# The place of two operand copies in the opening of a gated attention and GEGLU kernel

## The chip, the cores and the metric

The kernel runs on 1 core of one Trainium2 chip. The metric is device time in microseconds (us). Before the change the median of 3 runs was 596.25 us (595.72 to 597.62). The profile comes from one further execution, which took 596.87 us, with a span of 595.1 us from its first to its last instruction and a granted TensorE clock of 0.999.

The engines are named as in the profile: PE is TensorE's matmul and PEld its weight load, DVE is VectorE, ACT is ScalarE, POOL is GpSimd, SP is SyncE with its DMA queue.

## The reference

For 2048 tokens of width 512 the kernel mixes two branches with a gate per token:

```python
x = A_x
g = _sigmoid((x * gate_w).sum(-1, keepdims=True))
a = _A_ref(x, A_wqkv, A_wo)
b = _B_ref(x, B_w_gate, B_w_up, B_w_down)
return g * a + (1 - g) * b
```

Branch a projects x to queries, keys and values (32 heads of width 16). Each position attends to 8 positions, itself and every second one behind it; the result is projected with wo. Branch b is a GEGLU feed-forward layer of width 1792. All is float32.

## The kernel before

**Products.** Large matrix products are made from seven products of blocks instead of eight: x is cut in four blocks (a11, a12, a21, a22), a weight in four (b11, b12, b21, b22), and sums of blocks (s1 to s4 of x, t1 to t4 of the weight) are multiplied. `KEYS` lists the seven pairs for keys and queries: a11 x b11, a12 x b21, s2 x t2, s3 x t3, a22 x t4, s1 x t1, s4 x b22. Each operand of float32 is split in a high part, a copy to the type fp32r, and a low part, the raw value less the high part; a product of two operands is then three matmuls (high x high, low x high, high x low), for each of two chunks `kc` of the inner dimension. A copy of the high part is an ACT instruction, the low part a DVE subtraction.

**Token tiles and banks.** A block of x has four token tiles (`BT = 4`), and each tile of a product has a PSUM bank, 128 x 512. Products follow one another in the same bank: partial sums are evicted by an ACT copy when they stand for a result, and the next product accumulates on top.

**The opening** is written out at L1055 to L1197. The first two key products fill the banks `acc0` to `acc3` (`C`) and four `p` banks (`Z_`). `third(k)` (L1154) makes key product number k of `KEYS` on `C`, counted from 0: `third(2)` is the third product, s2 x t2; `third(3)` the fourth, s3 x t3; `third(4)` the fifth, a22 x t4. In `third`, each token tile's matmuls (`key_mm`, L454 to L461) are followed for k = 2 and 3 by an eviction on ACT (L1164) into a staging tile `hh` or `hl`, and by two stores on the SP queue (`store_b`, L463); for k = 4 by `take_first` (L320). The value products of the opening (`values`, L336, matmuls at L348) are interleaved: two of them ahead of `third(2)`, the others after the key products, beginning with s1 x t1.

**Copies and subtractions of the opening.** `late_split` (L1106) copies an operand's high part on ACT (L1108) and puts its low part on a list `low`; `lows(n)` (L1111) takes the first n from the list and issues their subtractions on DVE (L1114). `late_s` makes a sum of x, `late_b` a sum of the weight, both by `late_split`. In the profile t4's raw input is the tile `prod` and its parts lie in a tile `g` (g<-prod); s1's raw input is `lg` and its parts are in `S` (S<-lg); a22's parts are in `A`. `make_v` (L160) makes the operands of the value products in steps, taken one by one with `next(made)`: a copy at L87, a subtraction at L88, sums at L168.

**What sets the order.** A planner orders the instructions of each engine from the order of the text, their dependences and an estimated clock; an instruction whose inputs come early can go ahead of one that stands earlier in the text. Each engine then takes its instructions in the planned order. Two means hold an instruction: `tc.keep_in_program_order(ins)` puts `ins` behind the instruction of the same engine that precedes it in the text, without a wait of its own on the chip; `paced(ins)` (L581) does the same for DVE instructions while `PIN[0]` is true, which it is from L1073 to L1194, and ties an instruction to the last matmul while `PACING[0]` is true. ACT's copies of the opening have no hold.

**Later stages.** After the opening come the rest of the value products, the feed-forward loop of the first half of the tokens (`ffn(0)`, matmuls at L730 and L777) with the attention's DVE work spread over it (L519, L522, L558), then keys and values of the second half (`keys`, L416, and `values`), `ffn(1)` and the output. Weight operands `g` of the feed-forward layer are partly split by a DMA that adds raw to a negated copy (L689, issued from POOL, g<-raw).

## Time and profile before

| | us |
|---|---|
| runs, median of 3 | 596.25 (595.72 to 597.62) |
| profiled execution | 596.87 |
| its span | 595.1 |
| PE busy in the span | 586.6 |
| DVE busy | 533.3 |
| ACT busy | 429.4 |
| POOL busy | 123.4 |

The profile's views are read thus. The page gives busy time by engine. The list of waits gives, for an engine's line, what it waited for, the total, the number of times and the longest. A timeline is in the order of time, with equal neighbours merged: start and duration in us from the span's start, engine, line, operation, output<-input, shape, count, and in brackets the idle time of the engine before it with what ended it. A window gives the busy time of PE, PEld, DVE, ACT and POOL in a stretch, the granted clock, the mean busy share of the DMA engines and GB/s. The chain of waits follows back from the last instruction what released each step. A matmul's duration overlaps that of the next one, so steps of PE are read from start to start.

### The profile page before, as it was taken

The numbers are of one execution on the slowest core, as the hardware profiler recorded it, in microseconds if no ns is written. First come the engines' busy times: TensorE is split into PE (matmuls) and PEld (weight loads), VectorE is DVE, ScalarE is ACT, GpSimd is POOL, SyncE is SP. The second block draws the span as 40 slices with busy tenths as digits, with TensorE's granted clock in tenths as the row PEclk, the third lists the DMA queues.
The fourth block names the chain that finished last, engine by engine and source line by source line (L and its number), as shares of the span: only waits on it lengthen the run. The fifth ranks groups of instructions, "written<-read, shape, count | busy, mean of one in ns | idle before, by whom it ended". The sixth has DMA issues, their size and how long they took to land.

```text
span 595.1 us, 8276 instructions
## 1 busy us (share of the span) xinstructions
PE 586.6 (99%) x2743; PEld 488.8 (82%) x2743; DVE 533.3 (90%) x622; ACT 429.4 (72%) x758; POOL 123.4 (21%) x144
## 2 busy tenths in 40 slices
PE   9999999999999999999999999999999999999997
PEld 7889887888888888887788888888888888888885
DVE  6989898999799996999996999799979988999891
ACT  6778786678887779777767665767696778796632
POOL 0130670112111112112001571112121212141200
PEclk9999999999999999999999999999999999999999
DMA  8689999989878988899889999889778988988725
GB/s 301 223 235 295 307 284 236 295 245 243 260 219 246 232 268 234 237 344 267 255 264 330 258 276 227 230 190 265 198 247 213 260 213 215 265 197 230 98 53 176
DMA packets 89464, 143.28 MB, mean 241 GB/s; under 512 B 8655, under 2 KB 49999, under 8 KB 89422
## 3 DMA queue, kind: packets, MB, share of 16 engines
q1 hardware_dynamic: 67470, 106.91, 54.6%
q0 software_dynamic: 21664, 35.46, 33.8%
q8 instruction: 21, 0.34, 0.3%
q10 hardware_dynamic: 288, 0.39, 0.2%
q14 instruction: 21, 0.17, 0.1%
HBM read 69.83 MB, written 46.49 MB: 195 GB/s over the span
## 4 chain that ended last, share of the span: by engine, by line
PE 90%; DMA 6%; DVE 1%; ACT 1%; issue 1%; SPq 0%; ACTq 0%; DVEq 0%
PE p L730 42%; PE p L777 13%; PE acc L777 12%; PE acc L460 10%; PE p L1002 5%; PE acc L348 3%; PE p L348 3%; DMA g<-raw 2%; PE acc L1002 2%; DMA v<-vs 1%; DMA raw<-ws 1%; PE p L460 1%; DMA vs<-hh 1%; DMA raw<-xt 1%; DVE raw L245 1%
## 5 line engine op out<-in xcount | busy, mean ns | idle before, releaser
L730 PE MATMUL p<-S,g 128*128 128x512 f32 x672 | 166.7, 389 | 0.0
L730 PEld LDWEIGHTS p<-S,g 128*128 128x128 f32 x672 | 126.0, 188 | 26.1
L730 PE MATMUL p<-A,g 128*128 128x512 f32 x504 | 125.1, 390 | 0.7 <-DMA g<-raw 0.7
L730 PEld LDWEIGHTS p<-A,g 128*128 128x128 f32 x504 | 94.3, 188 | 20.8 <-DMA g<-raw 1.1
L558 DVE TENSOR_TENSOR prod<-v,lg 128x2048 f32<-128x2048 f32 x32 | 72.9, 2279 | 0.8
L519 DVE TENSOR_TENSOR prod<-kq 128x2048 f32<-128x2048 f32 x32 | 72.9, 2278 | 0.6 <-DMA kq<-kq 0.3
L522 DVE TENSOR_REDUCE lg<-prod 128x128 f32<-128x2048 f32 x32 | 73.0, 2281 | 0.1
L777 PE MATMUL p<-d,hh 128*128 128x512 f32 x224 | 68.8, 389 | 0.0
L689 POOL DMA_DIRECT2D g<-raw x27 | 23.4, 867 | 188.9 <-ACT g L686 122.9
L741 ACT ACTIVATE c<-p 128x512 f32<-128x512 f32 x56 | 33.3, 597 | 38.9 <-PE p L730 38.6
L777 PE MATMUL acc<-d,hh 128*128 128x512 f32 x224 | 58.4, 390 | 0.0
L777 PEld LDWEIGHTS acc<-d,hh 128*128 128x128 f32 x224 | 42.0, 188 | 8.9 <-ACT hh L749 0.2
L777 PEld LDWEIGHTS p<-d,hh 128*128 128x128 f32 x224 | 42.1, 188 | 8.7
L742 DVE TENSOR_TENSOR c<-c,s 128x512 f32<-128x512 f32 x56 | 37.8, 683 | 5.6 <-ACT c L741 5.4
L777 PE MATMUL p<-d,hl 128*128 128x512 f32 x112 | 42.6, 389 | 0.0
L746 DVE TENSOR_TENSOR c<-c 128x512 f32<-128x512 f32 x56 | 38.3, 684 | 3.2 <-ACT c L843 3.1
L562 DVE TENSOR_TENSOR prod<-prod 128x1024 f32<-128x1024 f32 x32 | 39.1, 1221 | 0.3
L735 ACT ACTIVATE s<-p 128x512 f32<-128x512 f32 x56 | 33.0, 590 | 7.1 <-PE p L730 6.5
L721 POOL DMA_DIRECT2D d<-r x23 | 19.7, 858 | 86.6 <-ACT d L720 60.0
L460 PE MATMUL acc<-d,S 128*128 128x512 f32 x144 | 35.2, 390 | 0.6 <-ACT hh L1164 0.6
L790 ACT ACTIVATE rt<-p 128x512 f32<-128x512 f32 x48 | 28.1, 594 | 9.4 <-PE p L777 9.1
L777 PE MATMUL acc<-d,hl 128*128 128x512 f32 x112 | 34.5, 389 | 0.0
(220 smaller groups left out, 1065.0 us busy)
## 6 DMA issues: line engine op xcount, KB each, us to landing
g<-raw POOLq DMA_DIRECT2D x27, 512.0 KB, 6.1
ws<-g SPq DMA_DIRECT2D x14, 768.0 KB, 5.9
g<-ws SPq DMA_DIRECT2D x14, 768.0 KB, 7.0
r<-wff SPq DMA_DIRECT2D x28, 256.0 KB, 4.5
raw<-wff SPq DMA_DIRECT2D x14, 512.0 KB, 4.5
d<-r POOLq DMA_DIRECT2D x23, 256.0 KB, 6.5
ws<-raw SPq DMA_DIRECT2D x14, 384.0 KB, 4.9
raw<-ws SPq DMA_DIRECT2D x14, 384.0 KB, 4.9
```

What stands on the lines that cost most here:

```text
L348: LAST[:] = [nc.tensor.matmul(ps[:, :n], x[:, ts], VO[b][w][:, kc * WQ:kc * WQ + n], start=first, stop=(kc == 1 and i == 2), skip_group_ch ...
L460: LAST[:] = [nc.tensor.matmul(ps, x[:, ts], w, start=(start and kc == i == 0), stop=(kc == 1 and i == 2), skip_group_check=True)]
L519: paced(nc.vector.tensor_tensor(prod, spans(k, jj), q[:, jj:jj + 2, None, :].to_broadcast([P, 2, W, UC]), op=OP.mult))
L522: nc.vector.tensor_reduce(two_of(lg, jj), prod.rearrange("p j w (h d) -> p (j w) h d", d=DH), axis=AX.X, op=OP.add)
L558: paced(nc.vector.tensor_tensor(prod.rearrange("p j w (h d) -> p (j w) h d", d=DH), spans(v, jj).rearrange("p j w (h d) -> p j w h d", d=D ...
L562: nc.vector.tensor_tensor(prod[:, :, :4], prod[:, :, :4], prod[:, :, 4:], op=OP.add)
L730: LAST[:] = [nc.tensor.matmul(ps, w_, a_, start=(start and kc == 0 and n == 0), stop=(kc == 1 and n == 2), skip_group_check=True)]
L741: nc.scalar.activation(c, ps, AF.Copy)
L742: nc.vector.tensor_tensor(c, c, s, op=OP.add)
L746: nc.vector.tensor_tensor(ge, ge, up, op=OP.mult)
L777: LAST[:] = [nc.tensor.matmul(pp, a[:, ts], w, start=(i == 0 and n == 0 and gr == 0), stop=(i == 1 and n == 2), skip_group_check=True)]
L1002: LAST[:] = [nc.tensor.matmul(pa, a, b, start=(first and n == 0), stop=(last and n == 2), skip_group_check=True)]
```

## The change

`late_split`, `late_s` and `late_b` take an optional hold for the high part's ACT copy. t4's two copies are given `tc.keep_in_program_order`; the ACT instruction ahead of the first in the text is the last eviction of `third(2)`. The call of `third(3)` is moved ahead of the s1 copies, which get the same hold; the ACT instruction ahead of the first of them is then the last eviction of `third(3)`. The subtractions of t4, a22 and s4, which were issued three and three around the s1 copies, are issued together ahead of `third(3)`. Those of s1 follow, as before, with `lows(len(low))` after the next step of `made`.

```diff
-    def late_split(name, kc, x):
+    def late_split(name, kc, x, hold=lambda ins: ins):
         hi, lo, raw = x
-        nc.scalar.activation(hi, raw, AF.Copy)
+        hold(nc.scalar.activation(hi, raw, AF.Copy))
         low.append((lo, raw, hi))
...
-    def late_s(n, kc):
+    def late_s(n, kc, *hold):
         i = {"s1": 3, "s2": 0, "s4": 1, "s3": 2}[n]
         raw = S1.pop(kc) if n == "s1" else XR[kc][:, i * 512:(i + 1) * 512]
         XOP[n, kc] = pair("S")
-        late_split(n, kc, (*XOP[n, kc], raw))
+        late_split(n, kc, (*XOP[n, kc], raw), *hold)
 
-    def late_b(n, kc):
-        late_split(n, kc, (*QO[n, kc], QR[n, kc]))
+    def late_b(n, kc, *hold):
+        late_split(n, kc, (*QO[n, kc], QR[n, kc]), *hold)
...
     for kc in range(2):
         combine_b("t4", "b21", "b21", "t2", kc)
-        late_b("t4", kc)
+        late_b("t4", kc, tc.keep_in_program_order)
         lows(1)
     for kc in range(2):
         late_split("a22", kc, (*X[0, 1, 2 + kc], XR[kc][:, 1536:]))
         sum_x(kc, "s4")
         late_s("s4", kc)
     set_x(0)
-    lows(3)
+    lows(min(6, len(low)))
+    third(3)
     for kc in range(2):
-        late_s("s1", kc)
-    lows(3)
-    third(3)
+        late_s("s1", kc, tc.keep_in_program_order)
     room_v(*LARGE)
     store_v()
     next(made)
```

## The prediction

> **What bounds the kernel now.** I read the page's busy shares first, then the list of what TensorE waited for, then the timelines of TensorE, ScalarE and VectorE around the edited lines, and last the chain of waits.

> ```profile
> span 595.1 us, 8276 instructions
> ...
> PE 586.6 (99%) x2743; PEld 488.8 (82%) x2743; DVE 533.3 (90%) x622; ACT 429.4 (72%) x758; POOL 123.4 (21%) x144
> ```

> TensorE (PE) is busy for 586.6 of 595.1 us. An edit to the order of the other engines can win only where it closes a gap of PE, and all its gaps together are 8.5 us. The waits of PE over the whole run, with the total, the number of times and the longest:

> ```profile
> PE p L730 <- DMA g<-raw: 0.7, 1, 0.7
> PE p L460 <- ACT p L434: 0.6, 1, 0.6
> PE acc L460 <- ACT hh L1164: 0.6, 1, 0.6
> PE acc L348 <- ACT hh L355: 0.5, 1, 0.5
> PE acc L460 <- ACT S L129: 0.4, 1, 0.4
> ```

> The third row is the opening's: a matmul of the key products (L460) waits once for an eviction (L1164). PE's timeline there (start, duration, engine, line, output<-input, count, and the idle time before it with what ended it), and then ScalarE's (ACT):

> ```profile
> 26.55 1.08 PE L460 MATMUL acc<-g,S 128*128 128x512 f32 x4
> 28.26 5.75 PE L460 MATMUL acc<-d,S 128*128 128x512 f32 x24 [0.62 <-ACT hh L1164]
> 33.84 5.60 PE L460 MATMUL acc<-g,A 128*128 128x512 f32 x24
> 39.28 3.44 PE L348 MATMUL p<-g,S 128*128 128x512 f32 x24
> ```

> ```profile
> 27.08 0.63 ACT L1108 ACTIVATE g<-prod 128x512 fp32r<-128x512 f32 x1
> 27.60 0.60 ACT L1164 ACTIVATE hh<-acc 128x512 f32<-128x512 f32 x1
> ...
> 29.04 0.63 ACT L1164 ACTIVATE hl<-acc 128x512 f32<-128x512 f32 x1
> 29.51 0.67 ACT L87 ACTIVATE g<-tb 128x516 fp32r<-128x516 f32 x1
> 30.04 0.67 ACT L1108 ACTIVATE g<-prod 128x512 fp32r<-128x512 f32 x1
> ...
> 31.08 0.64 ACT L1164 ACTIVATE hh<-acc 128x512 f32<-128x512 f32 x1
> ...
> 32.07 1.20 ACT L1108 ACTIVATE S<-lg 128x512 fp32r<-128x512 f32 x2
> 33.12 0.64 ACT L1164 ACTIVATE hl<-acc 128x512 f32<-128x512 f32 x1
> ...
> 34.07 0.67 ACT L1164 ACTIVATE hl<-acc 128x512 f32<-128x512 f32 x1
> 34.55 0.71 ACT L87 ACTIVATE g<-v 128x516 fp32r<-128x516 f32 x1
> ```

> The four rows of PE are the end of the third key product, the fourth (s3 x t3), the fifth (a22 x t4) and the value product s1 x t1. The third ends at 26.55 + 1.08 = 27.63. Its first eviction (27.60) stands on ACT behind one copy, t4's first (g<-prod, 27.08), and the fourth product, which goes on in the bank that is evicted, begins only at 28.26. PE stands for 0.62 us. The reader is to see that a copy needed only by the fifth product, at 33.84, went ahead of an eviction for which PE was waiting.

> **The change part by part.** No instruction is added, removed or resized. The two copies that get a hold issue no DMA, and the fourth product's stores keep their place among those of the Sync queue. What moves is the order of ACT's copies, and in the text the fourth product goes ahead of the s1 copies. VectorE's subtractions keep their sequence: two for t4, four for a22 and s4, then t1's, then two for s1.

> First edit: t4's first copy behind the third product's last eviction. That copy kept the eviction from ACT from 27.08 to 27.60, start to start, so 0.52 us. Without it the eviction takes the place at 27.08. From the eviction's start to PE's start it was 28.26 - 27.60 = 0.66 us, so the fourth product begins at 27.74, a gain of 0.52. The bounds: PE cannot gain more than the 0.62 us that it stood, and it gains nothing if another ready copy takes the free place. I take 0.52, since the eviction's input is there: of the four matmuls from 26.55 on the first ends about 0.4 us later (the 5.60 us row less 23 steps of 0.227, the step being (39.28 - 33.84) / 24), near 26.95. The second t4 copy has the hold too, but the ACT instruction ahead of it in the text is the first one, so its hold adds only their sequence.

> What becomes late is t4's copy itself. It now follows the fourth eviction, which moves from 29.04 to 28.52, so it starts near 29.04 instead of 27.08. Its subtraction stands on VectorE (DVE) ahead of others:

> ```profile
> 28.88 0.68 DVE L1114 TENSOR_TENSOR g<-prod,g 128x512 fp32r<-128x512 f32 x1
> 30.74 0.69 DVE L1114 TENSOR_TENSOR g<-prod,g 128x512 fp32r<-128x512 f32 x1 [1.18 <-ACT g L1108]
> ...
> 32.55 0.68 DVE L1114 TENSOR_TENSOR A<-raw,A 128x512 fp32r<-128x512 f32 x1
> ...
> 35.29 0.70 DVE L88 TENSOR_TENSOR g<-v,g 128x516 fp32r<-128x516 f32 x1 [0.85 <-ACT g L87]
> ...
> 40.70 0.70 DVE L88 TENSOR_TENSOR g<-tb,g 128x516 fp32r<-128x516 f32 x1 [0.90 <-ACT g L87]
> ```

> It goes from 28.88 to about 29.7, and the 1.18 us for which DVE stood before 30.74 covers these 0.8 us. The second t4 copy (30.04) has the same ACT work ahead of it as before: four evictions, t4's first copy, the value weight's copy of 29.51. So 30.74 and what follows stay. The fifth product reads them. It would begin at 33.84 - 0.52 = 33.32, and its fifth matmul, at 33.32 + 4 x 0.227 = 34.23, is the first that needs the second a22 low, done at 32.55 + 0.68 = 33.23: 1.0 us of cover. Beyond it every further us would stop PE one for one.

> Second edit: the s1 copies (32.07, two of them) go behind the eviction of 34.07, which moves to 33.55, so to 34.1, or to 34.6 if the value copy of 34.55 goes ahead of them. The eviction of 33.12 comes earlier, for which nobody waits: the fifth product comes to its bank at 33.32 + 6 x 0.227 = 34.68. The price is on DVE. If the s1 copies go first, t1's subtraction (35.29) comes about 0.5 us later, and the two of s1 behind it end at 37.6 instead of 37.1 (35.29 and three of 0.6). PE needs them from 39.28 - 0.52 = 38.76: 1.1 us of cover. Further down the 0.90 us for which DVE stood before 40.70 takes up the 0.5; without it the 0.5 would be paid. I take nothing, with 0 and +0.5 as the ends. The hold also keeps the s1 copies, whose inputs are early, from taking the place that t4's copy leaves.

> The sum at the opening is -0.52 + 0 + 0. It has to last to the end. The chain of waits shows the one place of the first hundred microseconds behind it where PE does not lead:

> ```profile
> 67.30 4.89 DMA vs<-hh
> ...
> 72.61 8.25 DMA v<-vs
> ...
> 81.10 10.90 DMA g<-raw
> ...
> 92.05 1.19 PE p L730 x4
> ```

> The chain reaches vs<-hh from PE's own work, so it should come 0.52 us earlier with PE, and the wait of 0.7 us at 92.05 should stay as long as it is. The profiled execution took 596.87 us, 1.77 more than its span and 0.62 more than the median of the runs, 596.25. By the sum it would take 596.35, and the median 595.73: I say 595.7. About 0.3%, 1.8 us, is what a measurement of this kernel can tell from no change, so the forecast is a gain too small to tell.

> **The rivals.** First: the gain is given back at 92.05, where PE comes 0.52 us earlier and g<-raw does not. [...]

> ```profile
> 68.25 2.29 DVE L519 TENSOR_TENSOR prod<-kq 128x2048 f32<-128x2048 f32 x1
> ...
> 68.87 4.06 POOL L465 DMA_DIRECT2D ks<-o  x1
> ...
> 79.48 2.28 DVE L522 TENSOR_REDUCE lg<-prod 128x128 f32<-128x2048 f32 x1
> ...
> 81.10 0.89 POOL L689 DMA_DIRECT2D g<-raw  x1 [1.99 <-DMA v<-vs]
> ```

> For it: one issue beside a DVE multiply took 4.06 us. Against it: the issue that matters took 0.89 us beside a reduction, and the profile has a transfer, not DVE, end the idle time before it. If it holds, the median stays at 596.25. [...]

> Second, slower than before: a transfer gets ahead of that chain. The window has DMA at 1.21 and 279 GB/s, and the issues are large:

> ```profile
> 75.00:90.00 15.00, 15.00 (x68) 12.44 (x67) 13.90 (x19) 12.47 (x20) 10.85 (x10) 1.00 1.21 279
> ```

> ```profile
> ws<-g SPq DMA_DIRECT2D x14, 768.0 KB, 5.9
> ```

> (The last three columns of the window are the granted clock, the DMA share and GB/s.) One such store of 768 KB more ahead of v<-vs or g<-raw takes 0.786 MB / 279 GB/s = 2.8 us. PE at 92.05 pays that in full, since it stands there already: -0.52 + 2.8 = +2.3, and the median comes to 598.5. For it: the order of the queues behind the edit is not written in the text but planned from an estimated clock, and 0.5 us can swap two issues that lie close. It eats the gain from a delay of 0.52 us on, and counts as slower from 2.3. Against it: a shift of everything by the same 0.52 swaps nothing.

> Third, faster: the new order closes other gaps as well. In the list above these are 0.7 at 92.05, and 0.6 and 0.4 before key products (L460) of the second pass, where the same kind of copies stands ahead of PE. All three with the 0.52 make 2.2, so 594.0. For it: they are of the same size and kind. Against it: no line there is edited, and it takes all of them to get past 1.8.

> Fourth: the change does not do what it says, because another copy takes the place at 27.08 (t4's copy alone has its input early there, and s1's is held). Then nothing moves: 596.25.

> **How the numbers follow.** The forecast has 0.36. Given back at 92.05: 0.10. Slower by a transfer: 0.30, of which 0.03 stays within 1.8 us. Faster by other gaps: 0.20, of which 0.03 stays within it. Without effect: 0.04. So faster by over 0.3% is 0.17, slower 0.27, and within it 0.36 + 0.10 + 0.04 + 0.03 + 0.03 = 0.56. The likeliest case alone would lie between 595.6 (the whole 0.62 gained) and 596.3 (0.5 paid for s1). The range reaches to 594.1 below, near the third rival's 594.0, and to 598.8 above, past the second's 598.5; with the rest of both beyond it, under 0.2 is left out.

> **What would show it.** Right: in ACT's timeline four L1164 rows follow one another from 27.1 on, with t4's first g<-prod near 29.0 and both S<-lg behind the last L1164 row near 34; the row "PE acc L460 <- ACT hh L1164: 0.6" shrinks to 0.1 or goes from PE's list; the fifth product begins near 33.3 with no wait in front of it; the value product p<-g,S near 38.8; and the wait at 92.05, then near 91.5, is still 0.7. Given back: that wait is 1.2. Slower: it is over 2, with another transfer ahead of v<-vs or g<-raw. Wrong in the first edit: another ACT row between 27.1 and the first eviction. Wrong in its cover: a wait of PE for a DVE subtraction at 33 to 35.

## The result: slower by 0.55%

| | before | changed |
|---|---|---|
| median of 6 runs, us | 596.93 (595.72 to 598.85) | 600.51 (600.28 to 601.39) |
| ratio to before | | 1.0055 (95% interval 1.0039 to 1.0070) |
| profiled execution, us | 596.87 | 600.28 |
| its span, us | 595.1 | 598.5 |

The forecast was 595.7 with a range of 594.1 to 598.8; the time lies above it. The page of the changed kernel and its list of what TensorE waited for:

```profile
span 598.5 us, 8269 instructions
...
PE 587.0 (98%) x2743; PEld 490.1 (82%) x2743; DVE 534.2 (89%) x622; ACT 427.7 (71%) x756; POOL 123.3 (21%) x144
```

```profile
PE p L460 <- ACT p L434: 3.4, 1, 3.4
PE p L73 <- DVE warm L70: 1.0, 1, 1.0
PE p L1002 <- ACT c L741: 0.9, 1, 0.9
PE p L730 <- DMA g<-raw: 0.9, 1, 0.9
```

PE's busy time is the same within 0.4 us; its waits are longer. The opening's row, hh L1164, is gone from the list. Against it stand +2.8 us in one wait of the second pass (0.6 before, 3.4 now), +0.9 before the output projection (L1002, no such row before), and some tenths at other places. This profile is of the one run of the six with a granted TensorE clock of 0.999; the other five had 0.993 to 0.997, and what that costs is read in the last section. The opening itself did what the prediction said, in ScalarE's and PE's timelines:

```profile
27.73 0.61 ACT L1164 ACTIVATE hh<-acc 128x512 f32<-128x512 f32 x1
...
29.16 0.65 ACT L1164 ACTIVATE hl<-acc 128x512 f32<-128x512 f32 x1
29.64 0.68 ACT L1108 ACTIVATE g<-prod 128x512 fp32r<-128x512 f32 x1
...
34.20 0.60 ACT L1164 ACTIVATE hl<-acc 128x512 f32<-128x512 f32 x1 [0.35 <-PE acc L460]
34.70 1.15 ACT L1108 ACTIVATE S<-lg 128x512 fp32r<-128x512 f32 x2
35.74 0.62 ACT L87 ACTIVATE g<-v 128x516 fp32r<-128x516 f32 x1
```

```profile
27.20 1.08 PE L460 MATMUL acc<-g,S 128*128 128x512 f32 x4
28.39 5.78 PE L460 MATMUL acc<-d,S 128*128 128x512 f32 x24
34.00 5.60 PE L460 MATMUL acc<-g,A 128*128 128x512 f32 x24
39.44 3.45 PE L348 MATMUL p<-g,S 128*128 128x512 f32 x24
```

From the start of the four matmuls to the start of the fourth product it is 28.39 - 27.20 = 1.19 us; before, 28.26 - 26.55 = 1.71. So 0.52 us are gone, to the hundredth what was forecast. The fourth product still begins at 28.39 in this execution, because the third ended 0.65 us later. The first loads came later: the first copy of ScalarE from a 128x512 tile of x (A<-raw, L87) starts at 7.61 with 1.00 us of waiting for raw<-xt, before at 6.89 with 0.16. In the repeat of the unchanged kernel below, the fourth product begins at 29.14.

The largest single loss is 250 us further on, where the first half of the tokens ends and the second begins. PE's timeline of the kernel before, then of the changed one (L777 is the last down projection, its operands hh and hl; L460 the first key products of the second half):

```profile
272.82 0.84 PE L460 MATMUL acc<-g,A 128*128 128x512 f32 x3
273.50 1.98 PE L777 MATMUL p<-d,hh 128*128 128x512 f32 x8
275.31 2.20 PE L460 MATMUL acc<-g,A 128*128 128x512 f32 x9
277.35 1.07 PE L777 MATMUL p<-d,hl 128*128 128x512 f32 x4
278.26 2.88 PE L460 MATMUL acc<-g,A 128*128 128x512 f32 x12
281.78 5.76 PE L460 MATMUL p<-d,A 128*128 128x512 f32 x24 [0.64 <-ACT p L434]
...
293.96 5.60 PE L460 MATMUL acc<-d,S 128*128 128x512 f32 x24
```

```profile
273.61 3.79 PE L460 MATMUL acc<-g,A 128*128 128x512 f32 x16
277.24 1.98 PE L777 MATMUL p<-d,hh 128*128 128x512 f32 x8
279.05 1.98 PE L460 MATMUL acc<-g,A 128*128 128x512 f32 x8
280.86 1.07 PE L777 MATMUL p<-d,hl 128*128 128x512 f32 x4
285.29 5.73 PE L460 MATMUL p<-d,A 128*128 128x512 f32 x24 [3.35 <-ACT p L434]
...
296.30 5.60 PE L460 MATMUL acc<-d,S 128*128 128x512 f32 x24
```

The same 36 matmuls stand in both ahead of the wait, in another order. Before, twelve key matmuls follow the four hl matmuls; in the changed kernel none do. Behind the hl matmuls ScalarE has to evict the four banks (L785) and copy the four first key sums to banks that they leave (L434), in the changed kernel:

```profile
281.29 0.69 ACT L785 ACTIVATE s<-p,gc 128x512 f32<-128x512 f32 x1 [4.86 <-PE p L777]
...
284.06 0.69 ACT L785 ACTIVATE c<-p,gc 128x512 f32<-128x512 f32 x1
284.62 1.58 ACT L434 ACTIVATE p<-acc 128x512 f32<-128x512 f32 x3
```

From the first eviction to the end of the first copy that is 281.29 to 285.2. Before, the twelve matmuls (2.72 us start to start) covered most of it; now PE stands 3.35 us.

The net loss of the place is smaller than this wait. From the first row shown to the fourth key product (acc<-d,S) it is 293.96 - 272.82 = 21.14 us before and 296.30 - 273.61 = 22.69 in the changed kernel: 1.55 us more. The wait is 2.7 us longer, but from 281.78 on the kernel before takes 12.18 us to the fourth key product, with two more waits of 0.4 and 0.2 (S L129, S L88), and the changed one takes 11.01 from 285.29, without them.

No line of the program there was edited. What changed is the planner's order. Of the instructions behind the opening that the first two experiments tie, so many stand out of the old sequence in the new one:

```
ACT 72 of 678   DVE 103 of 561   SP 31 of 331   PE 212 of 2538
```

With the fourth product's call moved in the text but neither hold, or with a hold on t4's second copy alone, the planned order behind the opening is the old one to the last instruction (read from the planned programs, which were not run). So it is the two holds that set off a new plan, each by itself, as the third and fourth experiments show on the chip.

### The profile page after: what moved, and what is told of

Its sections match the earlier page's. It is cut to its first block, busy times and chain, and to the rows that moved or that the text cites. A ratio compares the mean times of both kernels' runs of the same rounds, so it can differ in the third digit from the quotient of the medians.

```text
span 598.5 us, 8269 instructions
## 1 busy us (share of the span) xinstructions
PE 587.0 (98%) x2743; PEld 490.1 (82%) x2743; DVE 534.2 (89%) x622; ACT 427.7 (71%) x756; POOL 123.3 (21%) x144
## 4 chain that ended last, share of the span: by engine, by line
PE 86%; DMA 5%; issue 4%; ACT 4%; SPq 0%; POOL 0%; DVE 0%; POOLq 0%; ACTq 0%
PE p L730 38%; PE p L777 11%; PE acc L777 11%; PE acc L460 11%; PE p L1002 6%; PE acc L348 3%; PE p L348 2%; DMA g<-raw 2%; PE p L460 2%; PE acc L1002 2%; DMA hl<-c 1%; DMA raw<-ws 1%; DMA raw<-os 1%; PE p L73 1%; ACT g L686 0%
## 5 line engine op out<-in xcount | busy, mean ns | idle before, releaser
L730 PE MATMUL p<-S,g 128*128 128x512 f32 x672 | 167.0, 390 | 0.0
L730 PEld LDWEIGHTS p<-S,g 128*128 128x128 f32 x672 | 126.0, 188 | 25.9
L730 PE MATMUL p<-A,g 128*128 128x512 f32 x504 | 125.5, 390 | 0.9 <-DMA g<-raw 0.9
L730 PEld LDWEIGHTS p<-A,g 128*128 128x128 f32 x504 | 94.4, 188 | 20.8 <-DMA g<-raw 1.3
L519 DVE TENSOR_TENSOR prod<-kq 128x2048 f32<-128x2048 f32 x32 | 72.9, 2279 | 0.3
L522 DVE TENSOR_REDUCE lg<-prod 128x128 f32<-128x2048 f32 x32 | 73.0, 2281 | 0.1
L777 PE MATMUL p<-d,hh 128*128 128x512 f32 x224 | 68.5, 389 | 0.0
L741 ACT ACTIVATE c<-p 128x512 f32<-128x512 f32 x56 | 33.4, 596 | 37.7 <-PE p L730 37.7
L689 POOL DMA_DIRECT2D g<-raw x27 | 23.4, 866 | 178.1 <-ACT g L686 121.0
L777 PE MATMUL acc<-d,hh 128*128 128x512 f32 x224 | 58.4, 389 | 0.0
L777 PEld LDWEIGHTS p<-d,hh 128*128 128x128 f32 x224 | 42.1, 188 | 8.7
L777 PEld LDWEIGHTS acc<-d,hh 128*128 128x128 f32 x224 | 42.1, 188 | 8.7
L777 PE MATMUL p<-d,hl 128*128 128x512 f32 x112 | 42.6, 389 | 0.0
L460 PE MATMUL acc<-d,S 128*128 128x512 f32 x144 | 35.4, 391 | 0.1
L777 PE MATMUL acc<-d,hl 128*128 128x512 f32 x112 | 34.6, 391 | 0.2 <-DMA hl<-c 0.2
## 6 DMA issues: line engine op xcount, KB each, us to landing
ws<-g SPq DMA_DIRECT2D x14, 768.0 KB, 6.4
g<-ws SPq DMA_DIRECT2D x14, 768.0 KB, 7.0
```

What stands on the lines that cost most here:

```text
L460: LAST[:] = [nc.tensor.matmul(ps, x[:, ts], w, start=(start and kc == i == 0), stop=(kc == 1 and i == 2), skip_group_check=True)]
L519: paced(nc.vector.tensor_tensor(prod, spans(k, jj), q[:, jj:jj + 2, None, :].to_broadcast([P, 2, W, UC]), op=OP.mult))
L522: nc.vector.tensor_reduce(two_of(lg, jj), prod.rearrange("p j w (h d) -> p (j w) h d", d=DH), axis=AX.X, op=OP.add)
L730: LAST[:] = [nc.tensor.matmul(ps, w_, a_, start=(start and kc == 0 and n == 0), stop=(kc == 1 and n == 2), skip_group_check=True)]
L741: nc.scalar.activation(c, ps, AF.Copy)
L777: LAST[:] = [nc.tensor.matmul(pp, a[:, ts], w, start=(i == 0 and n == 0 and gr == 0), stop=(i == 1 and n == 2), skip_group_check=True)]
```

## The experiments

**The opening and the rest apart.** Two kernels tie the instructions that are traced behind the opening to a given sequence on each engine, by edges that order without a wait on the chip. The first has the changed text and the old sequence, the second the text of before and the new sequence.

```diff
+    PLANNED = {
...
+    }
+    made_now = {i.name: i for i in nc.cur_bb.bb.instructions}
+    for order in PLANNED.values():
+        last = None
...
+                if last is not None:
+                    tc.add_manual_dep(ins, last, mybir.DependencyInfo(mybir.DependencyClass.NoSync,
+                                      mybir.DependencyReason.DATA), reason="planned order")
+                last = ins.name
```

> The changed opening as it is, and behind the opening every instruction of each engine tied in the order that the kernel before had. Theory (the loss is in the new order that the planner made of the rest, and the opening itself gains): the fourth product's wait of 0.6 us is gone as in the changed kernel, PE's wait before the second pass's second key product is back from 3.4 to about 0.6 us, and the time is 0.3 to 0.7 us under the kernel before, near 596.4. Rival (the late t4 and s1 copies delay the operands or the DMA behind the opening, whatever the order): as slow as the changed kernel, near 600.5.

> The opening of the kernel before, and behind it every instruction of each engine tied in the order of the changed kernel. Theory (the new order of the rest costs about 4 us and the opening gains 0.5): 0.5 us over the changed kernel, near 601.0, with the 3.4 us wait before the second pass's second key product and the 0.9 us wait before the first output projection (L1002). Rival (the late copies of the opening are the cause): as the kernel before, near 597.

The new sequence behind the old opening is as slow as the change: ratio 1.0056 (1.0033 to 1.0078), with the 3.4 us wait:

```profile
PE p L460 <- ACT p L434: 3.4, 1, 3.4
...
PE acc L460 <- ACT hh L1164: 0.6, 1, 0.6
```

That fits the theory. The 0.9 us wait before L1002 did not come, so that one is not a property of the order. The new opening with the old rest was not the gain expected: 1.0026 (1.0005 to 1.0047). Its opening wait was gone and the boundary's back at 0.6, but PE stood 2.1 us at 93 us for g<-raw. Two loads of the next weights (L647), traced inside the opening and so not tied, had also moved, from among the fourth product's stores to behind them. That left open whether the copies, the loads or scatter were to blame.

**Each hold alone.** The first of the two kernels has the first line of this diff only, the second the rest of it (both with the new parameters of the helpers):

```diff
-        late_b("t4", kc)
+        late_b("t4", kc, tc.keep_in_program_order)
...
-    lows(3)
+    lows(min(6, len(low)))
+    third(3)
     for kc in range(2):
-        late_s("s1", kc)
-    lows(3)
-    third(3)
+        late_s("s1", kc, tc.keep_in_program_order)
```

> Only t4's copies are held; the text keeps the s1 copies ahead of the fourth product. Theory of the order: the opening's 0.6 us wait shrinks to 0.1 as in the changed kernel, and the planner makes yet another order of the rest, so the time can be anything between 596 and 601 and its waits lie at other places than in the opening. Rival that t4's lateness is what costs: near 600.5, with the 3.4 us wait. Rival that s1's hold is what costs: near 596.4.

> Only the fourth product's move and the hold on s1's copies; t4's first copy stays ahead of the third product's evictions. Theory of the order: the opening's wait stays at 0.6 us, and the rest is planned anew, with waits away from the opening and a time between 596 and 601. Rival that s1's hold is what costs: near 600.5 or 601. Rival that t4's lateness costs: near 597.

Both are slower than the kernel before: 1.0092 (1.0058 to 1.0126) and 1.0069 (1.0045 to 1.0092), medians 603.5 and 602.12 against 597.62. Their intervals overlap that of the change, so that they are worse than it is not shown. The times lie above the 596 to 601 that the theory gave, and the boundary's wait came again where other places were expected: both have the 3.4 us there, and waits of 1.9 and 2.4 us at 93 us. The opening's wait is gone with t4's hold alone, and is there at 0.6 with s1's. So the opening's wait and the time do not go together: a kernel that keeps the old wait of the opening loses as well. Each rival that blames one of the two copies by itself falls, since both kernels are slow.

**The copies alone, everything else as before.** As the first experiment, but with all that is traced behind the fourth product tied, and the fourth product's stores too, so that the L647 loads (527 and 529) stay where they were.

```diff
     PLANNED = {
...
-        'SP': '679 625 641-646 ...
+        'SP': '516-519 679 478-479 527 488-489 498-499 508-509 529 ...
```

> The text of the changed kernel, with every instruction traced behind the fourth product, and the fourth product's stores, tied in the order of the kernel before: only the ACT copies of t4, s4 and s1 (and some matmuls inside the fourth product) stand where the change puts them. In the first experiment the next weights' two loads had also moved behind the stores, and PE's wait at 92 us had grown from 0.7 to 2.1. Theory (that growth came with the moved loads or is scatter of the transfers there, not with the copies): the opening's wait is 0.1, the wait at 92 us near 0.7, the time 0.3 to 0.7 us under the kernel before. Rival (the copies themselves make the chain of transfers late): the wait at 92 us is 2 again, and the time 1.0 to 1.6 us over the kernel before.

> The kernel of the fifth experiment once more, for a second profile and a second interval. Theory: the opening's wait 0.1, the same waits elsewhere as the kernel before, 0.3 to 0.7 us under it, ratio 0.9988 to 0.9995; the first interval was 0.9955 to 1.0000. Rival (the first interval was scatter): ratio at 1.000 or over.

Ratios 0.9978 (0.9955 to 1.0000) and 0.9994 (0.9975 to 1.0013); medians 597.16 against 597.46 and 596.72 against 597.11, so 0.3 and 0.4 us less. A gain of half a microsecond fits, but the first interval reaches 1 and the second holds it, so it isn't proved by the times alone. A loss like that of the change is ruled out. The profile of the second:

```profile
PE p L73 <- DVE warm L70: 1.0, 1, 1.0
PE p L730 <- DMA g<-raw: 0.7, 1, 0.7
PE p L460 <- ACT p L434: 0.6, 1, 0.6
PE acc L348 <- ACT hh L355: 0.5, 1, 0.5
PE acc L460 <- ACT S L129: 0.4, 1, 0.4
```

```profile
26.77 1.08 PE L460 MATMUL acc<-g,S 128*128 128x512 f32 x4
27.96 5.75 PE L460 MATMUL acc<-d,S 128*128 128x512 f32 x24
33.55 5.60 PE L460 MATMUL acc<-g,A 128*128 128x512 f32 x24
38.99 3.44 PE L348 MATMUL p<-g,S 128*128 128x512 f32 x24
```

These are the first rows of before's list without that of hh L1164. The step from the four matmuls to the fourth product is 27.96 - 26.77 = 1.19 us again, the wait at 92 us is 0.7 again, and the span is 594.7 against 595.1. In the first of the two profiles the step and the wait at 92 us are the same, but a wait of 0.4 us before L1002 takes the gain back, and the span is 595.1. So the copies cost nothing where they went, and the opening gains the 0.52 us that were forecast; that this reaches the end fits the times and is not proved by them.

**The boundary repaired.** The changed kernel in its own sequence everywhere, except that the instructions traced about the boundary have the old one; then the same behind the old opening.

> The changed kernel in its own planned order everywhere but where the first half of the tokens ends and the second begins (about 262 to 300 us): there each engine has the order of the kernel before. Theory (the largest loss is a planned order in which VectorE and ScalarE make the last hidden block's parts late there): the 3.4 us wait of PE before the second key product of the second pass goes back to about 0.6, and the time falls by 2 to 3 us against the changed kernel, to 597.5 to 598.5. Rival (the wait follows from PE or DMA arriving at another time): the wait stays over 2 us and the time near 600.5.

> The opening of the kernel before, the rest in the order of the changed kernel, and its boundary of the two halves (262 to 300 us) in the order of the kernel before. In the second experiment this order without the repaired boundary had no wait at 92 us and none before the first output projection, but the 3.4 us wait and a slower clock behind it. Theory that the boundary carries that loss: 2.5 to 4.5 us under the second experiment, at or under the kernel before (596 to 598). Rival: near 600.

The first comes from 1.0055 down to 1.0021 (0.9999 to 1.0044), so about 0.34%, 2.0 us, with intervals that overlap a little; its median of 599.02 is above the 597.5 to 598.5 expected. Its list has no L434 row; in its place are two of 0.8 (S L88, S L129), and the wait at 92 us is 1.6. From the three key matmuls at 273.63 to the fourth key product at 296.33 it is 22.70 us, no less than the 22.69 of the changed kernel's first profile (in the second of the two it is 22.73). So the repair moves PE's waits and does not make the stretch shorter. What it gains is the clock: in the repeat of the changed kernel, with a granted clock of 0.50 for 3.41 us behind the wait, the same stretch takes 24.31 us (273.36 to 297.67). Nine of the twelve runs of each repaired kernel have a granted clock of 0.998 or more, and none of the twelve of the second experiment. The second is at 1.0027 (1.0003 to 1.0051): 1.7 us under its kernel with the unrepaired boundary, less than the 2.5 expected, within the two intervals' overlap, and not as fast as before. So the boundary is the largest part of the loss in a run in which the clock falls behind it (3.17 us, 24.31 less 21.14, of which 1.6 are the clock's); in the first profile of the change, with a whole clock, it is 1.55 of the 3.4 us, and the rest is spread over several places.

**Which engine's order.** The same repair for PE alone, and for all engines but PE:

> The changed kernel in its own order, and at the boundary of the two halves TensorE alone in the order of the kernel before: the four hl matmuls of the last down projection ahead of twelve key matmuls instead of behind all of them. Theory (the wait is PE's own order: behind the hl matmuls ScalarE needs 3.9 us for the evictions and bank copies, and PE has no matmul left to cover it): the 3.4 us wait goes to 0.6 to 1.0, but the hl matmuls come at about 277.8, and VectorE, in the new order, has hl ready only at about 279.4, so up to 1.6 us of wait appear in front of them; 0.5 to 1.5 us under the changed kernel. Rival (the late hh and hl parts on ScalarE and VectorE are the cause by themselves): the 3.4 us stay.

> The changed kernel in its own order, and at the same boundary every engine but TensorE in the order of the kernel before. Theory (PE's own order is the wait): the 3.4 us wait stays within 0.5, the time near 600.5. Rival (ScalarE's and VectorE's order is): the wait falls under 1.5 and the time under 599.

With PE alone repaired, PE's timeline is

```profile
274.58 0.84 PE L460 MATMUL acc<-g,A 128*128 128x512 f32 x3
277.45 3.69 PE L777 MATMUL p<-d,hh 128*128 128x512 f32 x8 [2.03 <-ACT hh L749]
...
287.47 4.83 PE L460 MATMUL p<-d,A 128*128 128x512 f32 x20 [0.64 <-ACT p L434]
```

and with all but PE:

```profile
282.56 1.07 PE L777 MATMUL p<-d,hl 128*128 128x512 f32 x4
286.99 5.19 PE L460 MATMUL p<-d,A 128*128 128x512 f32 x15 [3.35 <-ACT p L434]
```

The wait of 3.35 us is PE's own order: it stays to the hundredth when every other engine is put back, and goes to 0.64 when PE alone is. But PE's old order then meets ScalarE's new one, in which the last hh copy (L749) stands behind four bank evictions and two operand copies:

```profile
276.23 0.64 ACT L129 ACTIVATE d<-r 128x512 fp32r<-128x512 f32 x1
276.75 0.64 ACT L749 ACTIVATE hh<-c 128x512 fp32r<-128x512 f32 x1
```

So PE stands 2.03 us in front of the hh matmuls. The expectation had this wait at up to 1.6 us in front of the hl matmuls: the wrong operand. It also had a time under the changed kernel, which failed, as did the 600.5 expected of the other: 1.0092 and 1.0090, medians 603.45 and 603.06. At the boundary both have the half clock of the last section: the eight hh matmuls above took 3.69 us, where they took 1.98 before, and the 15 key matmuls 5.19, where 20 took 4.83 with PE alone put back. The rest are new waits. With PE alone put back they are 0.6 (c L741), 2.0 (hh L749) and 1.1 (S L129), with all but PE 0.5 (p L771), 0.3 (A L849) and 0.4 (S L129). PE's late hh and hl matmuls fit a plan in which hh is late on ScalarE, and undoing one of the two alone only adds waits. Why the planner's estimate made hh late was not tried.

**How far the kernels scatter.** The two kernels once more:

> The kernel before, unchanged, profiled once more: how far its waits and its step rate scatter from one execution to the next. If the wait at 92 us is a property of the order it is 0.5 to 1.0 again, and the opening's 0.6; if it is scatter of the transfers it differs by over 0.5 us. Where a wait of PE is over 3 us, the matmuls behind it may start every 0.43 us instead of 0.23 for some us; none is expected here, since no wait of this kernel is that long.

> The changed kernel, unchanged, profiled once more. If the 3.4 us wait belongs to its order it is there again within 0.2; the wait at 92 us and the one before the first output projection may scatter by over 0.5. Behind the 3.4 us wait the matmuls may start every 0.43 us for about eight of them, as in three other profiles with that wait, or every 0.23 as in the first of this kernel.

The unchanged kernel, in this execution with its opening 0.9 us late, has no wait at 92 us at all. The same six L730 matmuls that were parted by 0.69 us run through:

```profile
90.28 1.52 PE L730 MATMUL p<-S,g 128*128 128x512 f32 x6
91.64 1.64 PE L730 MATMUL p<-A,g 128*128 128x512 f32 x6
93.12 1.08 PE L777 MATMUL acc<-d,hh 128*128 128x512 f32 x4
```

So in this execution an opening that comes later is taken up by that wait, since the transfer doesn't come later with it: the third of the six, which waited for it until 92.05 before, starts here between 92.1 and 92.2 (an estimate: 91.64 and two steps of 0.227, and at most the 0.12 by which the row is longer than the 1.52 of six matmuls without a wait). The span is 595.6 against 595.1. The changed kernel has the 3.4 us wait again, and 1.4 us at 92 us; the wait before L1002 is not there. That one, 0.9 us in the first profile, is scatter: the kernel with the copies alone has it at 0.4 in one profile and not in the other.

## Why the prediction was wrong

- *What bounds the kernel, and where the opening loses.* Right. The wait on L1164 was the copy ahead of the eviction, and without it 0.52 us go.
- *t4's copy late, covered on VectorE.* Right. t4's first subtraction came at 30.35, or 29.70 without the 0.65 us by which this execution was late, where about 29.7 was forecast. In none of the profiles with t4's hold did PE wait for a subtraction between 33 and 35 us.
- *s1's copies behind the last eviction.* Right: they ran at 34.70, ahead of the value copy, and the value product began without a wait. The price taken, nothing, holds in the two experiments with the copies alone.
- *"The sum at the opening is -0.52 + 0 + 0. It has to last to the end."* This is where it failed. The sum left out a term: what the planner does to the rest when two instructions of the opening are held. By itself, behind the old opening, it measured +3.3 us (1.0056); the change is at +3.6, and the copies alone at about -0.4, which is not clear of nothing. About 1.7 us of it, in runs in which the clock falls once, is PE at half clock (an estimate: 3.41 us at a granted 0.50), for which the prediction had no term either. Already in the opening the Sync queue did not keep its order: the two loads of the next weights (L647) went behind the fourth product's stores.
- *The second rival.* It named the origin, "the order of the queues behind the edit is not written in the text but planned from an estimated clock", and put 0.30 on the slower side. But it gave the order one place and one mechanism, a transfer ahead of the chain to 92 us, and set against it that "a shift of everything by the same 0.52 swaps nothing". The holds do not shift everything by the same amount: they move ScalarE's copies against one another and against DVE and SP, and 212 matmuls left the old sequence. The largest price was at PE's own order at 281 us, a place that the prediction knew only as a wait of 0.6 us that might close. So the side was named, with a mechanism that did not come, and the range ended at 598.8.
- *Given back at 92.05.* Not this time: in both profiles of the copies alone the wait stays 0.7 and the gain passes this place. But the repeat of the unchanged kernel shows that its condition is real in the other direction.
- *Faster by other gaps.* The waits of 0.4 and 0.2 before the second pass's products did go in the changed kernel, as that rival thought possible, but behind a wait that had grown from 0.6 to 3.4; with the boundary repaired they are back, at 0.8 each.

## What to carry to other kernels

In a kernel whose queues are planned from an estimated clock, a hold is an edit to the whole plan. Compare the planned orders behind the edit before costing it, and give the replanning its own term, of the size of the waits that the old order happens to cover, not of the edit. Here that was 2.7 us of matmuls at one place, and 1.7 more where the clock fell behind it. To learn what an edit is worth by itself, tie the rest to the old sequence; here that turned +3.6 us into medians 0.3 and 0.4 us under before, not clear of no change.

## What the runs showed of the hardware

A wait of PE can cost more than its length. In the repeat of the changed kernel the matmuls behind the 3.4 us wait ran at a granted clock of 0.50 for 3.41 us (columns: PE, PEld, DVE, ACT, POOL busy, granted clock, DMA share, GB/s):

```profile
282.95:286.36 3.41, 1.32 (x6) 1.11 (x7) 3.41 (x6) 3.41 (x8) 1.63 (x3) 1.00 0.97 307
286.36:289.77 3.41, 3.41 (x10) 2.67 (x9) 3.41 (x7) 2.29 (x5) 0.00 (x0) 0.50 0.78 256
```

With PE's order alone put back, the eight hh matmuls at the half clock took 3.52 us start to start (277.45 to 280.97); the kernel before took 1.81 (273.50 to 275.31). By the granted 0.50, 3.41 us do the work of 1.7, so the wait costs 1.7 us on top (an estimate); measured, the stretch across the boundary took 24.31 us in the profile above and 22.69 in the first, 1.6 more. Five of the six profiles with the 3.4 us wait show the half clock, with 0.994 to 0.997 granted over the span; the first of the changed kernel, with 0.999, does not. The half clock also followed the 2.03 us wait of the kernel with PE's order alone, and the 2.4 us wait at 93 us of the kernel with s1's hold alone, where the next four matmuls took 2.04 us. It did not follow the 2.1 us wait at 93 us of the first experiment, where the next four took 1.20, nor shorter ones there: its granted clock is 1.000.

So the length of a wait alone does not tell whether the half clock follows. In the profile before and the first of the changed kernel the records of the granted clock show one stretch at full clock up to the last matmul, of 590.51 us, which is 173 times 3.413; the half-clock stretches in the repeat and with PE's order alone last 3.41. Counted off in windows of that length from the start of the full clock, the first profile of the changed kernel, the kernel with PE's order alone and the first experiment read:

```profile
280.07:283.48 3.41, 1.86 (x9) 1.21 (x7) 3.15 (x4) 2.19 (x4) 0.65 (x2) 1.00 0.55 167
283.48:286.89 3.41, 1.60 (x7) 1.35 (x8) 3.41 (x7) 3.41 (x8) 1.51 (x3) 1.00 0.99 272
```

```profile
274.09:277.50 3.41, 1.38 (x7) 0.81 (x5) 3.41 (x5) 3.30 (x7) 2.35 (x4) 1.00 1.09 323
277.50:280.91 3.41, 3.41 (x8) 2.74 (x9) 3.41 (x6) 0.00 (x0) 0.00 (x0) 0.50 1.05 414
```

```profile
89.85:93.26 3.41, 1.55 (x7) 0.94 (x5) 2.23 (x4) 3.38 (x5) 0.00 (x0) 1.00 1.26 202
```

The runs' times show the price too. In the three later series the kernel before ran 74 times; 65 runs with a granted clock of 0.998 to 1.000 took 595.6 to 600.0 us, with a median of 597.4, and the nine with 0.993 to 0.997 took 599.3 to 603.3.
